# Log-forget running sum placed first in the order, w_in handed out later and shared by two blocks, V's high part on ScalarE

## The chip, the cores and the metric

The kernel runs on one core of a Trainium2 chip. The metric is device time of one execution in microseconds (us); it is the median of several runs. The engines are TensorE (PE, with its weight loads as PEld), VectorE (DVE), ScalarE (ACT), GpSimd (POOL) and SyncE (SP). SP's queue issues nearly all DMAs here. Every engine and every queue works through its own instructions in a fixed order, and an instruction that waits holds all that stand behind it.

## The reference

Attention with a decay, then two feed-forward layers, all in float32 (the weights are kept as float64 pairs and decoded on the chip):

```python
# q, k, v: (4, 8, 576, 64); f: (4, 8, 576)
scores = q @ k.T / sqrt(64)
cum = cumsum(log(clip(f, 1e-4, 1)), -1)
scores = where(causal, -1e9, scores + cum[:, :, :, None] - cum[:, :, None, :])
x = softmax(scores) @ v               # reshaped to 2304 tokens x 512
h = x @ w_in                          # 512 x 2048
y = (h * tanh(softplus(h))) @ w_out   # 2048 x 512
g = maximum(y @ w1, y @ w2, y @ w3)   # 512 x 768 each
out = g @ w_out2                      # 768 x 512
```

## The kernel before, in words

Every large product is done in three matmuls of split values (high x high, high x low, low x high; `mm3`). `split` makes the high part by a rounding copy on a named engine and the low part by a subtraction on another.

**Attention** goes over 16 pairs of heads; each pair has two *units* (`g` = 0 for query rows 0 to 255, `g` = 1 for rows 256 to 575). Here the 32 units are counted 0 to 31, so that pair p has units 2p and 2p+1. `load` issues the DMAs of a pair (q, k, v into `rawq`, `rawk`, `rawv`, one buffer each, and the running sum `cum_d`, spread over partitions, into `cb`). `prep` splits them and turns q and k by PE transposes (`tr`). `scores` makes matmuls into `sc`, then one DVE instruction each (L391) that adds the decay and takes the minimum (`mn`), an exponential on ACT (L397), and a scaling of P on POOL (L404). `av`, which runs one unit later, turns P (`pp`), splits it into TA or TB and multiplies by V; its sums go by way of `xt` (L453) and an SP DMA (L461) to the DRAM tensors `x_d`. A pair's `prep` stands between the two units of the pair before.

**The running sum** is made once: f is loaded into `fl` (L122), clipped (L125), its logarithm taken on ACT (L126), summed along the row on DVE (L128), scaled (L129) and stored as `cum_d` (L130). Every `cb` load reads `cum_d`.

**w_in** is loaded by a generator, `load_w_in`: 16 half column groups, two to a group `fp` of 256 columns. A half group is two DMAs into `wr` (L149), one ACT instruction (L152), four DVE instructions (L155, L158, L161, L165, 64 in all), the high part on ACT (L135) and the low part on POOL (L141). Two staging buffers (`wt`, `wr`) hold them.

**h** = x w_in is done in 72 steps, each one block of 256 tokens (`i`, 9 of them) by one column group (`fp`, 8 of them), 24 matmuls a step. A block can start when its tokens of all heads are stored; blocks 0 and 1 become ready in the course of units 6 to 8, block 6 only near the end of attention.

The order of instructions is set by the tile scheduler. The loop at L535 calls the attention generator once per unit under `tc.high_priority(AHEAD)`, then hands out one half group of w_in, then up to four h steps. What has higher priority is put first where it fits.

When attention is over, its SBUF is given to w_out (`wo`), which is decoded on DVE while the last 24 h steps run; then come y and the second layer.

Of the kernel before, what the change touches and what calls it, by code (L numbers as in the profile page):

```python
# [9 lines left out]
F32 = mybir.dt.float32  # L10
# [3 lines left out]
AF = mybir.ActivationFunctionType  # L14
ALU = mybir.AluOpType
# [16 lines left out]
AHEAD = 3000  # L32
# [35 lines left out]
def tile_decay_attention__mish_ff__max3_ff(  # L68
# [16 lines left out]
    nc = tc.nc  # L85
    B, H, S, D = q.shape
# [3 lines left out]
    NH = B * H  # L90
    KD = DM // 128
    NFP = DFF // 256
    NF2 = DFF2 // 128
    NBLK = NT // BLK
    scale = 1.0 / float(D) ** 0.5
# [8 lines left out]
    cum_d = dram.tile([NH, S], F32, name="cum_d")  # L104
# [7 lines left out]
    with tc.tile_pool(name="setup", bufs=1) as sp:  # L112
        maskf = sp.tile([128, 128], F32, name="maskf")
        nc.gpsimd.memset(maskf, 0.0)
        nc.gpsimd.affine_select(
            out=maskf, in_=maskf, pattern=[[-1, 128]], compare_op=ALU.is_ge,
            fill=-1e30, base=0, channel_multiplier=1,
        )
        for rows, cols in ((slice(0, 64), slice(0, 64)), (slice(64, 128), slice(64, 128))):
            nc.vector.tensor_copy(mask4[rows], maskf[rows, cols])  # L120
        fl = sp.tile([NH, S], F32, name="fl")
        nc.sync.dma_start(fl, f.rearrange("b h s -> (b h) s"))  # L122
        one = sp.tile([NH, S], F32, name="one")
        nc.vector.memset(one, 1.0)
        nc.vector.tensor_scalar(fl, fl, 1e-4, 1.0, op0=ALU.max, op1=ALU.min)  # L125
        nc.scalar.activation(fl, fl, AF.Ln)  # L126
        cum = sp.tile([NH, S], F32, name="cum")
        nc.vector.tensor_tensor_scan(cum, one, fl, 0.0, op0=ALU.mult, op1=ALU.subtract)  # L128
        nc.vector.tensor_scalar(cum, cum, 1.0 / scale, None, op0=ALU.mult)  # L129
        nc.sync.dma_start(cum_d[:], cum)  # L130
        nc.scalar.preload_act_table_set("natural_log_exp_and_others")

    def split(dst_hi, dst_lo, src, eng_hi, eng_lo):
        if eng_hi == "act":
            nc.scalar.activation(dst_hi, src, AF.Copy)  # L135
        elif eng_hi == "pool":
            nc.gpsimd.tensor_scalar(dst_hi, src, 1.0, 1.0, op0=ALU.mult, op1=ALU.mult)
        else:
            nc.vector.tensor_copy(dst_hi, src)
        eng = nc.gpsimd if eng_lo == "pool" else nc.vector  # L140
        eng.tensor_tensor(out=dst_lo, in0=src, in1=dst_hi, op=ALU.subtract)  # L141
# [32 lines left out]
    def mm3(ps, whl, xhl, start, stop):  # L174
        (wh, wl), (xh, xl) = whl, xhl
        nc.tensor.matmul(ps, wh, xh, start=start, stop=False, skip_group_check=True)  # L176
        nc.tensor.matmul(ps, wh, xl, start=False, stop=False, skip_group_check=True)  # L177
        nc.tensor.matmul(ps, wl, xh, start=False, stop=stop, skip_group_check=True)  # L178
# [11 lines left out]
    def load_w_in():  # L190
        for fp in range(NFP):
            fs = slice(fp * 256, fp * 256 + 256)
            for c in range(0, KD, 2):
                blocks = [moe_w_in[d * 128:(d + 1) * 128, fs] for d in (c, c + 1)]
                load_split(
                    wst, wi[fp][:, 0, c:c + 2], wi[fp][:, 1, c:c + 2], blocks, "act", "pool", abs_eng="act"
                )
                yield
            loaded.add(fp)

    def load_x(i):
        xr = xp.tile([128, KD, BLK], F32, name="xr", tag="xr", bufs=1)
        nc.sync.dma_start(xr, x_d[i][:])
        xh = xp.tile([128, KD, BLK], F32R, name="xh")
        xl = xp.tile([128, KD, BLK], F32R, name="xl")
        split(xh, xl, xr, "pool", "pool")
        return xh, xl
# [9 lines left out]
    def att_psum(name):  # L217
        return aps.tile([128, 512], F32, name=name, tag="ps", bufs=4)
# [5 lines left out]
    raw = [ap_.tile([128, 640 if c == "v" else S], F32, name=f"raw{c}") for c in "qkv"]  # L224

    qk = [ap_.tile([128, 9, 3 - i, 64], F32R, name=f"qk{i}") for i in range(2)]
    vs = [aw.tile([128, 10, 2, 64], F32R, name=f"vs{i}") for i in range(2)]
# [33 lines left out]
                src[b, hs, 512:S, :].rearrange("h p d -> p h d"),  # L261
            )

    def split_raw(t, r):

        split(t[:, :, 0], t[:, :, 1], r.rearrange("p (n d) -> p n d", d=64), "dve", "pool")

    def load(b, hp):

# [39 lines left out]
    def prep(J):  # L309

        qh = as_.tile([128, 2, 512], F32R, name="qh", bufs=2)
        ql = as_.tile([128, 2, 512], F32R, name="ql", bufs=2)
        kk = as_.tile([128, 2, S], F32R, name="kT", bufs=2)
        last = q4[count["prep"] % 2]
        count["prep"] += 1

        def turn(dst, c, src):
            nc.tensor.transpose(dst[:, c:c + 128].bitcast(F32R), src, identr)

        rest = att_psum("tr")  # L320

        split_raw(qk[1], raw[1])
        split_raw(qk[0], raw[0])
        nc.gpsimd.tensor_scalar(
            qk[0][:, :, 2], raw[0].rearrange("p (n d) -> p n d", d=64), 1.0, 1.0, op0=ALU.mult, op1=ALU.mult
        )
        for i, part, dst, n in ((1, 0, kk, 0), (0, 0, qh, 1), (0, 1, ql, 2)):
            src = lambda blk: qk[i][:, blk, part:part + 2, :].rearrange("p a d -> p (a d)")
            for h in range(2):
                tr = att_psum("tr")  # L330
                for c in range(4):
                    turn(tr, c * 128, src(4 * h + c))
                nc.scalar.activation(
                    dst[:, h, 0:512].rearrange("p (c t) -> p c t", t=4),
                    tr.rearrange("p (t c) -> p c t", t=4),
                    AF.Copy,
                )
            turn(rest, n * 128, src(8))
        rr = rest[:, 0:384].rearrange("p (i h c) -> p i h c", i=3, h=2)
        nc.scalar.activation(kk[:, :, 512:S], rr[:, 0], AF.Copy)  # L340
        for a in range(2):
            nc.scalar.activation(
                last[:, a].rearrange("p (a c) -> p a c", c=64)[:, 0:4:3, :], rr[:, 1 + a], AF.Copy
            )
        split_raw(J["vs"], raw[2])
        J.update(q=(qh, ql), q4=last, k=kk)

    def score_mm(J, h, qt, dst, c0, w):
# [142 lines left out]
    def ready(i):  # L491
        return BLK * (i + 1) <= done

    def h_steps():


        half = NFP // 2
        order = [(i, fp) for fp in range(half) for i in (0, 1)]
        order += [(i, fp) for i in (0, 1) for fp in range(half, NFP)]
        order += [(i, fp) for i in range(2, NBLK) for fp in range(NFP)]  # L500
        final = {i: n for n, (i, _) in enumerate(order)}
        xs = {}
        asked = 0
        for n, (i, fp) in enumerate(order):
            while not ready(i):
                yield False

            while asked < NBLK and ready(asked) and asked <= i + 1 and (asked < 2 or n > final[asked - 2]):
                xs[asked] = load_x(asked)
                asked += 1  # L510
            while fp not in loaded:
                next(wgen, None)
            xh, xl = xs[i]
            h = hps.tile([128, 2, BLK], F32, name="h")
            for a in range(2):
                fs = slice(a * 128, (a + 1) * 128)
                for c in range(KD):
                    mm3(
                        h[:, a, :], (wi[fp][:, 0, c, fs], wi[fp][:, 1, c, fs]),
                        (xh[:, c, :], xl[:, c, :]), a == 0 and c == 0, c == KD - 1,  # L520
                    )
            he = hst.tile([128, 2, BLK], F32, name="he")
            if n % 2 and done < NT:
                nc.vector.tensor_copy(he, h)
            else:
                nc.scalar.activation(he, h, AF.Copy)  # L526
            ib, off = divmod(i * BLK, BLK2)
            nc.sync.dma_start(h_d[ib][fp][:, :, off:off + BLK], he)
            yield True

    wgen = load_w_in()
    attn = attention()
    steps = h_steps()
    credit = 0.0
    while True:  # L535

        with tc.high_priority(AHEAD):
            done = next(attn, None)
        if done is None:
            break  # L540
        next(wgen, None)
        credit += RATE
        while credit >= 1.0:
            credit -= 1.0
            if not next(steps, False):
                credit = 0.0
# [69 lines left out]
    for step, (ib, fp, a) in enumerate(todo):  # L616
        n = blocks1[ib][1]
# [103 lines left out]
```

## Time and profile before

| | us |
|---|---|
| median of 3 runs | 1052.75 (1051.04 to 1054.09) |
| profiled execution | 1048.8 |
| its span | 1047.0 |
| PE busy in the span | 958.4 |
| DVE busy | 524.3 |
| ACT busy | 415.4 |
| POOL busy | 381.0 |

The profiled execution is a little faster than the three timed ones. Its time is 1.8 us longer than its span. A busy time is a sum over stages that have different limits, so the stages have to be looked at one by one.

### The profile page before, as it was taken

The numbers are of one execution on the slowest core, as the hardware profiler recorded it, in microseconds if no ns is written. First come the engines' busy times: TensorE is split into PE (matmuls) and PEld (weight loads), VectorE is DVE, ScalarE is ACT, GpSimd is POOL, SyncE is SP. The second block draws the span as 40 slices with busy tenths as digits, with TensorE's granted clock in tenths as the row PEclk, the third lists the DMA queues.
The fourth block names the chain that finished last, engine by engine and source line by source line (L and its number), as shares of the span: only waits on it lengthen the run. The fifth ranks groups of instructions, "written<-read, shape, count | busy, mean of one in ns | idle before, by whom it ended". The sixth has DMA issues, their size and how long they took to land.

```text
span 1047.0 us, 15897 instructions
## 1 busy us (share of the span) xinstructions
PE 958.4 (92%) x5756; PEld 848.4 (81%) x5756; DVE 524.3 (50%) x1119; ACT 415.4 (40%) x920; POOL 381.0 (36%) x437
## 2 busy tenths in 40 slices
PE   2666779999998999999699989998999999999998
PEld 2555669999998999899688778777988888888886
DVE  5898854565556555578865775653211111112110
ACT  2667655655655655542124344433221211211111
POOL 5766665445644652255433333330111001011010
PEclk9887789999999899989999999998999999999999
DMA  5654443445443431285644665543300100200101
GB/s 150 200 157 137 132 132 103 129 118 161 136 127 123 121 117 63 78 301 183 191 136 161 208 194 172 191 147 111 105 22 0 61 21 1 71 11 1 41 0 41
DMA packets 106446, 119.16 MB, mean 114 GB/s; under 512 B 33984, under 2 KB 79552, under 8 KB 106368
## 3 DMA queue, kind: packets, MB, share of 16 engines
q1 hardware_dynamic: 106368, 118.15, 36.2%
q8 instruction: 45, 0.74, 0.3%
q14 instruction: 33, 0.27, 0.1%
HBM read 85.01 MB, written 33.10 MB: 113 GB/s over the span
## 4 chain that ended last, share of the span: by engine, by line
PE 56%; DMA 17%; DVE 16%; POOL 4%; issue 3%; SPq 2%; ACT 2%; POOLq 0%; DVEq 0%; ACTq 0%
PE g L178 7%; PE g L177 7%; PE g L176 7%; DMA wr<-in_moe_w_dram 5%; DMA wr<-in_moe_w_out_dram 4%; PE av L436 4%; PE h L176 4%; PE h L177 4%; DMA cb<-cum_d 4%; PE pp L423 4%; PE h L178 4%; PE sc L356 3%; DVE wt L161 3%; PE o L176 2%; PE o L178 2%
## 5 line engine op out<-in xcount | busy, mean ns | idle before, releaser
L176 PE MATMUL h<-xh,wi 128*128 128x256 f32 x576 | 167.5, 292 | 9.9 <-ACT he L526 8.5
L177 PE MATMUL h<-xl,wi 128*128 128x256 f32 x576 | 167.8, 291 | 1.9 <-POOL xl L141 1.9
L178 PE MATMUL h<-xh,wi 128*128 128x256 f32 x576 | 167.0, 290 | 0.0
L141 POOL TENSOR_TENSOR hl<-mx,hh 128x512 fp32r<-128x512 f32 x27 | 36.4, 1349 | 278.7 <-ACT hh L135 278.7
L177 PE MATMUL g<-yl,wm 128*128 128x512 f32 (+1 forms) x360 | 134.8, 374 | 0.0
L176 PE MATMUL g<-yh,wm 128*128 128x512 f32 (+1 forms) x360 | 134.7, 374 | 0.0
L178 PE MATMUL g<-yh,wm 128*128 128x512 f32 (+1 forms) x360 | 134.6, 374 | 0.0
L176 PE MATMUL y<-gh,wo 128*128 128x512 f32 (+1 forms) x320 | 118.2, 373 | 5.8 <-ACT gh L135 4.6
L177 PE MATMUL y<-gl,wo 128*128 128x512 f32 (+1 forms) x320 | 119.3, 374 | 3.3 <-DVE gl L141 3.1
L176 PEld LDWEIGHTS h<-xh,wi 128*128 128x128 f32 x576 | 111.3, 194 | 11.2 <-ACT he L526 8.7
L178 PE MATMUL y<-gh,wo 128*128 128x512 f32 (+1 forms) x320 | 118.1, 371 | 0.0
L177 PEld LDWEIGHTS h<-xl,wi 128*128 128x128 f32 x576 | 111.9, 194 | 3.1 <-POOL xl L141 2.1
L178 PEld LDWEIGHTS h<-xh,wi 128*128 128x128 f32 x576 | 111.8, 194 | 0.7
L607 ACT ACTIVATE g<-g 128x512 f32<-128x512 f32 (+1 forms) x80 | 46.8, 588 | 128.9 <-DMA g<-h_d 110.7
L677 DVE TENSOR_TENSOR mx<-g,mx 128x512 f32<-128x512 f32 x27 | 18.7, 693 | 156.2 <-PE g L178 156.2
L423 PE MATMUL pp<-ident,P 128*128 128x128 f32 x320 | 71.9, 321 | 23.0 <-POOL P L404 21.8
L397 ACT ACTIVATE P<-P,mn 128x128 f32<-128x128 f32 (+3 forms) x128 | 71.3, 558 | 48.7 <-DVE mn L391 48.0
L177 PEld LDWEIGHTS g<-yl,wm 128*128 128x128 f32 x360 | 68.2, 190 | 13.2
L178 PEld LDWEIGHTS g<-yh,wm 128*128 128x128 f32 x360 | 68.2, 189 | 13.1
L176 PEld LDWEIGHTS g<-yh,wm 128*128 128x128 f32 x360 | 68.2, 189 | 13.0
L404 POOL TENSOR_SCALAR P<-P,rr 128x256 f32<-128x256 f32 (+3 forms) x128 | 69.2, 559 | 23.9 <-ACT vlo L444 11.0
L141 DVE TENSOR_TENSOR gl<-g,gh 128x512 fp32r<-128x512 f32 (+1 forms) x80 | 60.9, 766 | 33.0 <-ACT gh L135 32.5
(101 smaller groups left out, 1995.9 us busy)
## 6 DMA issues: line engine op xcount, KB each, us to landing
h_d<-he SPq DMA_DIRECT2D x72, 256.0 KB, 3.3
g<-h_d SPq DMA_DIRECT2D x64, 256.0 KB, 3.2
wr<-in_moe_w_out_dram SPq DMA_DIRECT2D x22, 512.0 KB, 4.1
wr<-in_moe_w_dram SPq DMA_DIRECT2D x24, 384.0 KB, 3.2
wr<-in_moe_w_in_dram SPq DMA_DIRECT2D x32, 256.0 KB, 3.1
cb<-cum_d SPq DMA_DIRECT2D x64, 128.0 KB, 3.3
cb<-cum_d SPq DMA_DIRECT2D x32, 144.0 KB, 3.7
xr<-x_d SPq DMA_DIRECT2D x9, 512.0 KB, 3.7
```

Of the source, the lines that this page charges most:

```text
L141: eng.tensor_tensor(out=dst_lo, in0=src, in1=dst_hi, op=ALU.subtract)
L161: nc.vector.scalar_tensor_tensor(out=ti, in0=hi, scalar=-0x40000000, in1=ti, op0=ALU.bitwise_and, op1=ALU.bitwise_or,)
L176: nc.tensor.matmul(ps, wh, xh, start=start, stop=False, skip_group_check=True)
L177: nc.tensor.matmul(ps, wh, xl, start=False, stop=False, skip_group_check=True)
L178: nc.tensor.matmul(ps, wl, xh, start=False, stop=stop, skip_group_check=True)
L356: nc.tensor.matmul(o, lhs, rhs, start=n == 0, stop=n == len(mms) - 1, skip_group_check=True)
L397: nc.scalar.activation(Pt, Pt, AF.Exp, scale=-1.0, bias=mn[:, cl:cl + 1], accum_out=sm[:, ci:ci + 1],)
L404: nc.gpsimd.tensor_scalar(Pt, Pt, rr[:, ci:ci + 1], 1.0, op0=ALU.mult, op1=ALU.mult)
L423: nc.tensor.transpose(pp[:, n * 128:n * 128 + 128], Pt[:, k0:k0 + 128], ident)
L436: nc.tensor.matmul(avp[h][:, off:off + w], vl, T[:, i, c:c + w], start=kt == 0 and i == 0 and not (g == 0 and h == 1), stop=last and i == ...
L607: nc.scalar.activation(g, g, AF.Mish)
L677: nc.vector.tensor_tensor(out=mx, in0=g[1], in1=mx, op=ALU.max)
```

## The change

Four edits. The running sum's instructions get the highest priority of all. w_in is handed out two half groups at a time in calls 7 to 14 of the loop (call n+2 carries unit n) in place of one in every call from the first; h steps may still ask for a group earlier. The first six column groups of blocks 0 and 1, in place of the first four, alternate between the two blocks. V's high part is made by ACT in place of DVE.

```diff
-        fl = sp.tile([NH, S], F32, name="fl")
-        nc.sync.dma_start(fl, f.rearrange("b h s -> (b h) s"))
...
-        nc.sync.dma_start(cum_d[:], cum)
+        with tc.high_priority(2 * AHEAD):
+            fl = sp.tile([NH, S], F32, name="fl")
+            nc.sync.dma_start(fl, f.rearrange("b h s -> (b h) s"))
+            one = sp.tile([NH, S], F32, name="one")
+            nc.vector.memset(one, 1.0)
+            nc.vector.tensor_scalar(fl, fl, 1e-4, 1.0, op0=ALU.max, op1=ALU.min)
+            nc.scalar.activation(fl, fl, AF.Ln)
+            cum = sp.tile([NH, S], F32, name="cum")
+            nc.vector.tensor_tensor_scan(cum, one, fl, 0.0, op0=ALU.mult, op1=ALU.subtract)
+            nc.vector.tensor_scalar(cum, cum, 1.0 / scale, None, op0=ALU.mult)
+            nc.sync.dma_start(cum_d[:], cum)
...
-    def split_raw(t, r):
+    def split_raw(t, r, eng="dve"):
 
-        split(t[:, :, 0], t[:, :, 1], r.rearrange("p (n d) -> p n d", d=64), "dve", "pool")
+        split(t[:, :, 0], t[:, :, 1], r.rearrange("p (n d) -> p n d", d=64), eng, "pool")
...
-        split_raw(J["vs"], raw[2])
+        split_raw(J["vs"], raw[2], "act")
...
-        half = NFP // 2
+        half = NFP - 2
...
-    credit = 0.0
+    credit, na = 0.0, 0
     while True:
...
-        next(wgen, None)
+
+        na += 1
+        for _ in range(2 if 7 <= na <= 14 else 0):
+            next(wgen, None)
```

In the changed program the lines behind L121 have a number higher by one (by four behind the loop).

**SP's queue at the start.** Before, the load of f and the store of the sum stand behind the loads of two pairs and of part of a third (`raw*` are q, k and v, `wr` is w_in):

```order
L122 DMA fl<-in_f_dram 32x576
L149 DMA wr<-in_moe_w_in_dram 128x512 x2
L247 DMA rawq<-in_q_dram 128x2x256
...
L247 DMA rawq<-in_q_dram 128x2x256
L252 DMA rawq<-in_q_dram 64x64 x2
L255 DMA rawv<-in_v_dram 128x4x64 x2
L259 DMA rawv<-in_v_dram 64x2x64
L130 DMA cum_d<-cum 32x576
L149 DMA wr<-in_moe_w_in_dram 128x512 x2
L281 DMA cb<-cum_d 128x256
```

Now the queue begins like this:

```order
L123 DMA fl<-in_f_dram 32x576
L248 DMA rawk<-in_k_dram 128x2x256
L253 DMA rawk<-in_k_dram 64x64 x2
L248 DMA rawq<-in_q_dram 128x2x256
L253 DMA rawq<-in_q_dram 64x64 x2
L256 DMA rawv<-in_v_dram 128x4x64
L131 DMA cum_d<-cum 32x576
L256 DMA rawv<-in_v_dram 128x4x64
L260 DMA rawv<-in_v_dram 64x2x64
L282 DMA cb<-cum_d 128x256
```

The sum and the `cb` loads of the first pair have moved ahead of the loads of the second pair, which now come behind them; the first w_in load stands behind the `x_d` store of unit 0.

**DVE at the start and in unit 1.** Before, the start of DVE's program reads (`qk_188` and `qk_187` are split k and q, `vs` split V, `identr` what the transposes need, `mask` a causal mask):

```order
L139 CAST qk_188<-rawk 128x9x64
L139 CAST qk_187<-rawq 128x9x64
L109 CAST identr<-ident 128x128
L120 CAST mask_122<-maskf 64x64 x2
L139 CAST vs_189<-rawv 128x10x64
L139 CAST qk_188<-rawk 128x9x64
L125 TENSOR_SCALAR fl<-fl 32x576
L128 SCALAR_TENSOR_TENSOR cum<-one,fl 32x576
L129 TENSOR_SCALAR cum<-cum 32x576
```

and now:

```order
L126 TENSOR_SCALAR fl<-fl 32x576
L129 SCALAR_TENSOR_TENSOR cum<-one,fl 32x576
L140 CAST qk_188<-rawk 128x9x64
L130 TENSOR_SCALAR cum<-cum 32x576
L109 CAST identr<-ident 128x128
L120 CAST mask_122<-maskf 64x64 x2
L140 CAST qk_187<-rawq 128x9x64
L392 ISA P_0_311,mn<-sc,cb 128x128
```

q's cast now stands behind the sum and behind the two mask casts. Further down, in the scores of unit 1, before (`wt` is w_in):

```order
L391 ISA P_0_418,mn<-sc,cb 128x384
L391 ISA mn 128x1
L391 ISA P_0_424,mn<-sc,cb 128x512
L391 ISA mn 128x1
L155 TENSOR_SCALAR wt<-wt 128x512
L391 ISA P_1_430,mn<-sc,cb 128x384
L391 ISA mn 128x1
L158 TENSOR_SCALAR wt<-wt 128x512
L391 ISA P_1_436,mn<-sc,cb 128x512
L391 ISA mn 128x1
L161 SCALAR_TENSOR_TENSOR wt<-wr,wt 128x512
L155 TENSOR_SCALAR wt<-wt 128x512
```

and now:

```order
L140 CAST qk_188<-rawk 128x9x64
L392 ISA P_0_396,mn<-sc,cb 128x384
L392 ISA mn 128x1
L140 CAST qk_187<-rawq 128x9x64
L392 ISA P_0_402,mn<-sc,cb 128x512
L392 ISA mn 128x1
L392 ISA P_1_408,mn<-sc,cb 128x384
L392 ISA mn 128x1
L392 ISA P_1_414,mn<-sc,cb 128x512
L392 ISA mn 128x1
L392 ISA P_None,mn<-sc,cb_225 128x288
L392 ISA mn 128x1
```

The w_in instructions have gone from these scores, and the casts of the pair after next (pair 2) stand there.

**SP's queue at the end of attention.** Before (`x_d_68` is the last store of attention, `xr` the load of a block of x for h):

```order
L461 DMA x_d_67<-xt_5869 128x64
L461 DMA x_d_68<-xt_5869 128x256
L203 DMA xr<-x_d_67 128x1024
L149 DMA wr<-in_moe_w_out_dram 128x1024
L149 DMA wr<-in_moe_w_out_dram 128x1024
```

and now:

```order
L462 DMA x_d_67<-xt_5845 128x64
L462 DMA x_d_68<-xt_5845 128x256
L150 DMA wr<-in_moe_w_out_dram 128x1024
L204 DMA xr<-x_d_67 128x1024
L150 DMA wr<-in_moe_w_out_dram 128x1024
```

The first load of w_out has moved ahead of the load of block 7. Over the whole program, counted in the order of each engine:

| ahead of the end of unit | 1 | 3 | 5 | 7 | 9 | 10 |
|---|---|---|---|---|---|---|
| w_in instructions on DVE (of 64), before | 26 | 44 | 59 | 64 | 64 | 64 |
| now | 6 | 20 | 33 | 44 | 59 | 64 |

| h steps on PE ahead of the end of unit | 9 | 14 | 15 | 21 | 22 | 29 | 31 |
|---|---|---|---|---|---|---|---|
| before | 1.5 | 14.0 | 16.0 | 30.4 | 32.0 | 46.2 | 48.0 |
| now | 1.3 | 15.0 | 16.1 | 31.0 | 32.0 | 47.0 | 48.0 |

From the end of unit 31 on, PE's program is the same in both.

## Rows read from the trace of the kernel before

**Rows 1.** Page, part 1: busy time, share of the span, instructions.

```profile
PE 958.4 (92%) x5756; PEld 848.4 (81%) x5756; DVE 524.3 (50%) x1119; ACT 415.4 (40%) x920; POOL 381.0 (36%) x437
```

**Rows 2.** Windows of 25 us: busy us and instructions by engine, granted clock, DMA.

```profile
50.00:75.00 25.00, 18.28 (x102) 14.73 (x100) 24.38 (x55) 17.20 (x44) 16.13 (x16) 0.84 0.48 137
...
125.00:150.00 25.00, 21.91 (x139) 19.63 (x137) 16.40 (x48) 16.32 (x44) 16.66 (x20) 0.80 0.38 113
...
275.00:300.00 25.00, 25.00 (x213) 24.82 (x212) 13.80 (x41) 14.93 (x39) 10.82 (x18) 1.00 0.41 126
```

**Rows 3.** Timeline, first 30 us: start, duration (us), engine, instruction, idle before.

```profile
0.73 0.44 SPq L247 DMA_DIRECT2D rawk<-in_k_dram  x1
...
5.89 0.75 DVE L139 CAST qk<-rawq 128x576 fp32r<-128x576 f32 x1 [1.17 <-DMA rawq<-in_q_dram]
...
6.97 2.62 DVE L120 CAST mask<-maskf 64x64 bf16<-64x64 f32 x2 [0.19 <-POOL maskf L115]
...
9.62 0.50 DVE L139 CAST vs<-rawv 128x640 fp32r<-128x640 f32 x1
...
10.70 1.38 DVE L125 TENSOR_SCALAR fl<-fl 32x576 f32<-32x576 f32 x1
...
13.32 0.58 PE L356 MATMUL sc<-kT,qh 128*128 128x256 f32 x1 [1.40 <-ACT qh L333]
...
14.58 0.74 DVE L129 TENSOR_SCALAR cum<-cum 32x576 f32<-32x576 f32 x1
...
29.25 0.29 DVE L391 CUSTOM_DVE_ANT_0 P<-sc,cb 128x128 f32<-128x128 f32 x1 [0.90 <-POOL cb L284]
```

**Rows 4.** The chain of waits, 0 to 66 us: start, us, what held the chain.

```profile
21.91 2.06 DMA cum_d<-cum
...
24.04 0.33 SPq L281
...
33.97 1.73 PE sc L356 x4
```

**Rows 5.** Timeline, ends of units 1, 3, 5, 7 (SP's stores) and 9 (DVE).

```profile
63.59 0.81 SPq L461 DMA_DIRECT2D x_d<-xt  x2
...
94.51 0.81 SPq L461 DMA_DIRECT2D x_d<-xt  x2
...
120.28 0.89 SPq L461 DMA_DIRECT2D x_d<-xt  x2
...
143.86 0.80 SPq L461 DMA_DIRECT2D x_d<-xt  x2
...
167.66 0.61 DVE L453 TENSOR_TENSOR xt<-av,vlo 64x64 f32<-64x64 f32 x3
```

**Rows 6.** Groups of instructions on DVE, 8 to 130 us: busy us, mean ns.

```profile
L165 DVE SCALAR_TENSOR_TENSOR wt<-wr,wt 128x512 int32<-128x512 int32 x16 | 14.3, 893 | 0.1
L161 DVE SCALAR_TENSOR_TENSOR wt<-wr,wt 128x512 int32<-128x512 int32 x16 | 13.8, 863 | 0.1
L158 DVE TENSOR_SCALAR wt<-wt 128x512 int32<-128x512 int32 x16 | 12.5, 781 | 0.2
...
L155 DVE TENSOR_SCALAR wt<-wt 128x512 f32<-128x512 f32 x16 | 8.6, 536 | 9.0 <-ACT wt L152 9.0
...
L139 DVE CAST vs<-rawv 128x640 fp32r<-128x640 f32 x5 | 5.2, 1044 | 0.1
```

**Rows 7.** Groups of instructions on ACT, 8 to 130 us.

```profile
L135 ACT ACTIVATE wi<-wt 128x512 fp32r<-128x512 f32 x16 | 10.1, 629 | 17.0 <-DMA cum_d<-cum 8.8 <-DVE wt L165 8.1
```

**Rows 8.** Who waited for whom, PE, 140 us to the end: us, times, longest.

```profile
PE pp L423 <- POOL P L404: 9.4, 7, 4.0
PE h L176 <- ACT he L526: 8.5, 1, 8.5
```

**Rows 9.** The chain of waits, 436 to 450 us.

```profile
444.03 2.35 POOL xl L141
...
446.81 4.56 DMA wr<-in_moe_w_out_dram
```

More of the change, by code (lines that the diff above doesn't have):

```diff
@@ L120, in tile_decay_attention__mish_ff__max3_ff @@
             nc.vector.tensor_copy(mask4[rows], maskf[rows, cols])
-        fl = sp.tile([NH, S], F32, name="fl")
-        nc.sync.dma_start(fl, f.rearrange("b h s -> (b h) s"))
[L123 to L129, printed above, removed]
-        nc.sync.dma_start(cum_d[:], cum)
+        with tc.high_priority(2 * AHEAD):
[9 more added lines that the diff above has]
+            nc.sync.dma_start(cum_d[:], cum)
         nc.scalar.preload_act_table_set("natural_log_exp_and_others")
```

## The prediction

> **What bounds the kernel now.** I read the page's busy times first, then windows of 25 us, then the chain of waits, then the timelines of the first 170 us. PE is busy for 958.4 of 1047.0 us [rows 1], so the profile's page alone says that PE is the bound and that a change to loads and casts is worth little. The windows say otherwise for the beginning: from 50 to 75 us PE is busy for 18.28 of 25 us at a granted clock of 0.84, while DVE is busy for 24.38; from 275 to 300 us PE is busy throughout at 1.00 and DVE for only 13.80 [rows 2]. So the first 170 us, eight to ten units of attention with no h step to fill PE, are paced by other engines, and behind them PE is nearly full: from 140 us on it waits only for some 9.4 us on P and once for 8.5 us [rows 8]. What a change takes from the first 170 us is therefore kept, unless it is given back in one of these later waits.
>
> In the first 170 us the reader is to see two things. The first score reaches DVE at 29.25 us, though the first score matmul starts at 13.32 [rows 3]: between them the chain goes through the store of `cum_d`, issued at 21.91, and the `cb` loads from 24.04 [rows 4]. DVE had the sum ready at 15.32 (14.58 + 0.74); the store waited 6.6 us in SP's queue behind loads of later pairs. Second, the ends of units 1, 3, 5, 7 and 9 lie at 63.6, 94.5, 120.3, 143.9 and 168.3 us [rows 5]: a pair takes 30.9, 25.8, 23.6 and 24.4 us, and in these four stretches DVE has 18, 15, 5 and 0 instructions of w_in.
>
> **The change part by part.**
>
> *A, the sum first.* Two things must now be ready for the first score. One is `cb`. f is issued in the place of the first load, 0.73 us; with the 2.06 us of the store of `cum_d` as its landing [rows 3, 4] it is there at about 2.8. From the clip to the end of the scale it took 4.6 us (10.70 to 15.32), and the cast of k (0.75) now stands in between: 8.2. The store lands 2.1 later, and from the first `cb` load to the first score on DVE it took 5.2 us (24.04 to 29.25) [rows 3, 4]: 15.5. The other is q. Its cast now stands behind the scale and the two mask casts (2.62 us [rows 3]): it starts at about 10.9. From q's cast to the first score matmul it took 7.4 us (5.89 to 13.32), and two matmuls of 0.58 more to the first score's end: 19.4. But in these 7.4 us ACT held q's copies behind the logarithm, which now comes long before; the idle time ahead of the matmul, 1.40 us [rows 3], shows at least that much, and on an otherwise empty DVE the clip and the masks should be shorter. I take 16.9, between the two and nearer to the first. Gain 12.4 us, bounds 9.9 and 13.8.
>
> *B, units 0 and 1 without w_in.* By the order 26 w_in instructions stood ahead of the end of unit 1, and now 6. One costs DVE 0.77 us ((14.3 + 13.8 + 12.5 + 8.6) / 64 [rows 6]). What of that lies on the path I read from the pairs: 18 against 5 instructions is 30.9 against 23.6 us, 0.56 us each; 15 against 5 is 0.22 each [rows 5]. So 20 fewer are worth 11.2 us (4.4 to 15.4). Against it stand two new waits. The loads of pair 1's k and q now come behind `cb`: twelve issues at some 0.45 us [rows 3] from 10.4 on, q's last is issued at about 16, lands at 18, and its preparation (7.4 us as above) ends at 25.4; PE has unit 1's scores queued behind those transposes. That is 8.5 us behind the first score, where it was 4.7 (29.25 to 33.97 [rows 3, 4]): 3.8 lost. And DVE now has pair 2's casts among unit 1's scores; the one of q waits for a load that can only be issued when pair 1's q has been split: one landing, 2.1. Sum of B: 11.2 - 5.9 = 5.3 us gained, bounds 1.5 lost and 9.5 gained.
>
> *C, units 2 to 9.* Now 14, 13, 11 and 15 w_in instructions stand in the four pairs. Pairs with 15 took 25.8 us, with 5, 23.6 [rows 5]; so I give them 25.6, 25.3, 24.9 and 25.9, together 101.7 against 104.7 before. Gain 3 us. If each of the 15 instructions more (53 against 38) costs 0.56, it is a loss of 8; the bound on the other side is 6 gained. The cast of V is in it: it leaves DVE and costs ACT about 0.63 us (0.629 for 512 columns [rows 7]), which is hidden, since ACT is busy for only 17.20 of 25 us [rows 2].
>
> V's cast took 0.50 us at 9.62, where POOL stood idle, and 1.044 in the mean of five [rows 3, 6]; the five cost 2.5 us of DVE by the short duration and 5.2 by the mean. The Trainium skill, "SBUF — State Buffer", section "Who interferes with whom", says that VectorE in certain modes and GpSimd take one pair of SBUF ports in turn, each for a whole instruction, and that ScalarE has ports of its own. By that rule the long casts were waits that ScalarE will not have, C would be 2.7 us better and the time 1032; by the short row alone it stays at 1034.
>
> *D, h steps that run ahead.* In the order h is 1.0 step ahead at unit 14, 0.6 at unit 21, and 0.8 at unit 29, and then must wait for the same blocks. A step is 24 matmuls; PE does 213 in 25 us where it is full [rows 2], so 2.8 us. At units 22 and 23 and at units 30 and 31 PE then has 0.6 and 0.8 steps less to fill with, where it already waits for P [rows 8]: 3.9 us lost, at the least none. The sharing itself removes and adds no instruction. w_in is not late for h: 59 of 64 instructions stand ahead of unit 9's end, and the steps done by then use group 0 alone.
>
> *E, w_out's first load.* It was issued at 446.81 behind a load of x that waited for POOL's 2.35 us [rows 9]; it now stands ahead of that load. From there to the end of h the w_out load is what the h stores queue behind. Gain 2 us, at the least none.
>
> Sum: 12.4 + 5.3 + 3.0 - 3.9 + 2.0 = 18.8 us. The profiled execution took 1048.8 us, so it would be 1030.0. The median of the runs is 3.95 above the profiled one; the forecast for the median is 1052.75 - 18.8 = 1034.0.
>
> **The rivals.**
>
> *w_in was on the path in full.* Each of its 20 instructions in units 0 and 1 is worth 0.77 us, V's five casts are worth their mean (2.7 more in C), and h running ahead costs half: 12.4 + 15.4 - 5.9 + 5.7 - 2 + 2 = 27.6 us, 1025. For it: DVE at 24.38 of 25 [rows 2]. Against it: the pair with 5 instructions took only 2.2 us less than the one with 15.
>
> *Only the sum counts.* Units are held by `cb`, SP's queue and POOL's order, not by DVE: B is its lower bound, 1.5 lost, C nothing, D as above, E nothing: 12.4 - 1.5 - 3.9 = 7.0 us, 1046. For it: the same 2.2 us, and POOL at 16 to 17 us in both early windows [rows 2].
>
> *The load returns as h starts (slower).* In units 6 to 10 31 w_in instructions now stand where 5 stood, and DVE holds P, x and the first h copies behind them. 26 more, each at a price on the path, stand against 12.4 + 5.3 + about 4 of units 2 to 5, less the 3.9 of D: 17.8 us. It turns at 0.68 us each; at 0.77 it is 2.2 us slower, at the longest of the means, 0.89 [rows 6], 5.4 us: 1058. Against it: DVE is busy for only 16.40 of 25 us from 125 to 150 us [rows 2].
>
> *The change does nothing.* The first score is held by q until close to 29 us and B fails: within 3 us of before. Nothing in the rows speaks for it; q's path would have to be 10 us longer.
>
> **How the numbers follow.** Forecast 60 in 100, w_in in full 16, only the sum 16, slower 5, nothing 3. The first three are faster by more than 0.3% (3.2 us), about what a measurement can tell from no change: 0.92 faster, 0.03 same, 0.05 slower. The range takes in the first two rivals: 1023 to 1046.
>
> **What would show it.** A: the first L392 on DVE at about 17 us. B: unit 1's `x_d` store at about 46 us, pair 1's transposes at 20 to 25. C: unit 9's end at about 148 us, pairs of 25 to 26 us. D: the waits of PE for P longer by 2 us at units 22 and 23, and again before the end of attention. E: the first w_out load right behind the last `x_d` store, some 19 us earlier than 446.8. It would be wrong if P or `xt` waits in units 6 to 9 for w_in on DVE, or if the second and third pair's loads hold units 1 to 3 by more than 6 us.

## The result

| | before | after |
|---|---|---|
| median of the runs made together | 1053.42 (1051.04 to 1055.08) | 1038.31 (1036.30 to 1042.16) |
| profiled execution | 1048.8 | 1036.78 |
| its span | 1047.0 | 1034.9 |

The ratio is 0.9879, 95% interval 0.985 to 0.9907: faster by a little over 1%, some 15 us between the medians, 12.1 us between the two spans of the profiled executions, which all stages below are read from. The forecast was 1034.0 in 1023 to 1046, with 18.8 us between the profiled executions. The direction and the range hold; between the profiled executions 6.7 us of the sum are missing.

### The profile after

The page's busy times answer to [rows 1]; they say as little as before:

```profile
PE 957.5 (93%) x5756; PEld 844.8 (82%) x5756; DVE 509.5 (49%) x1103; ACT 425.6 (41%) x936; POOL 379.9 (37%) x437
```

The timeline of the first 15 us, to be read against [rows 3] (start, duration, engine, instruction, idle time before and what ended it):

```profile
2.60 0.45 DVE L126 TENSOR_SCALAR fl<-fl 32x576 f32<-32x576 f32 x1 [1.10 <-DMA fl<-in_f_dram]
...
6.17 0.34 SPq L131 DMA_DIRECT2D cum_d<-cum  x1
...
7.41 0.89 DVE L120 CAST mask<-maskf 64x64 bf16<-64x64 f32 x2
7.92 0.40 SPq L282 DMA_DIRECT2D cb<-cum_d  x1
8.33 0.75 DVE L140 CAST qk<-rawq 128x576 fp32r<-128x576 f32 x1
...
12.95 0.76 PE L357 MATMUL sc<-kT,qh 128*128 128x256 f32 x2
...
14.30 0.29 DVE L392 CUSTOM_DVE_ANT_0 P<-sc,cb 128x128 f32<-128x128 f32 x1 [5.22 <-PE sc L357]
```

The first score is on DVE at 14.30 where it was at 29.25, and it now waits for PE's scores, no longer for `cb`. The ends of units 1, 3, 5 and 7 (SP's stores), of unit 9 (DVE) and of unit 10 (SP), and the last store of attention with the first w_out load behind it, from the timeline, against [rows 5, 9]:

```profile
46.47 0.47 SPq L462 DMA_DIRECT2D x_d<-xt  x1
...
70.51 0.81 SPq L462 DMA_DIRECT2D x_d<-xt  x2
...
96.98 0.81 SPq L462 DMA_DIRECT2D x_d<-xt  x2
...
121.48 0.80 SPq L462 DMA_DIRECT2D x_d<-xt  x2
...
149.88 1.10 DVE L454 TENSOR_TENSOR xt<-av,vlo 64x320 f32<-64x320 f32 x4
...
163.47 0.80 SPq L462 DMA_DIRECT2D x_d<-xt  x2
...
430.40 0.80 SPq L462 DMA_DIRECT2D x_d<-xt  x2
431.30 0.37 SPq L150 DMA_DIRECT2D wr<-in_moe_w_out_dram  x1
```

In the kernel before, the end of unit 10 and the last store of attention read

```profile
184.11 0.80 SPq L461 DMA_DIRECT2D x_d<-xt  x2
...
444.05 0.80 SPq L461 DMA_DIRECT2D x_d<-xt  x2
```

The lead over before is 15.0 us at the first score, 17.1 at unit 1, 24.0 at unit 3, 23.3 at unit 5, 22.4 at unit 7, then only 17.3 at unit 9, but 20.6 again at unit 10. At the end of attention it is 13.7, at the end of h (534.8 before, 521.8 after) 13.0, at the end of the span 12.1. So more was gained early than forecast, and it was given back at two places. One is units 8 and 9, which take 29.5 us (121.48 to 150.98) where they took 24.4; two thirds of this is made good by the end of unit 10. The other, and the larger one, is behind unit 10: 6.9 us. Windows of 25 us (busy time of PE, PEld, DVE, ACT, POOL, then granted clock and DMA), against [rows 2]:

```profile
50.00:75.00 25.00, 18.95 (x108) 15.46 (x107) 22.01 (x56) 18.95 (x48) 19.42 (x22) 0.84 0.52 148
...
125.00:150.00 25.00, 19.90 (x129) 18.13 (x130) 21.85 (x45) 16.95 (x42) 19.33 (x22) 0.80 0.47 145
...
225.00:250.00 25.00, 22.38 (x163) 22.07 (x163) 10.02 (x35) 12.68 (x34) 13.14 (x15) 0.86 0.50 150
250.00:275.00 25.00, 25.00 (x212) 24.82 (x211) 13.89 (x38) 15.30 (x38) 13.98 (x18) 1.00 0.44 132
```

From 125 to 150 us DVE has 21.85 us of work where it had 16.40: w_in's decoding now lies there. From 225 to 250 us PE does 163 matmuls where a full window has 212. The chain of waits there (start, us, what held the chain):

```profile
219.14 4.07 DMA x_d<-xt
223.27 3.96 DMA xr<-x_d
227.27 0.11 issue
227.38 1.06 POOL xh L138
228.44 0.04 issue
228.48 0.50 PE h L177 x2
...
235.65 0.21 PE h L179
235.87 0.19 PE h L177
236.06 0.12 PE h L178
```

The first h step of block 2 stands ahead of attention's matmuls on PE, and PE waits 2.62 us for its x, which has just gone out to DRAM and come back. Behind the wait an h matmul takes 0.21 us until 235.9 and 0.12 us from then on; the granted clock of the window is 0.86. By an estimate from these rows the 2.6 us wait cost some 6 us (49 matmuls of 0.12 us fewer than in a full window): to the wait come some 7 us, 229 to 236 us, at a granted clock of 0.50 to 0.54, the lower of the two levels.

### The profile page after: what moved, and what is told of

Same layout as the page of the kernel before. It is cut to its first block, busy times and chain, and to the rows that moved or that the text cites. A ratio compares the mean times of both kernels' runs of the same rounds, so it can differ in the third digit from the quotient of the medians.

```text
span 1034.9 us, 15873 instructions
## 1 busy us (share of the span) xinstructions
PE 957.5 (93%) x5756; PEld 844.8 (82%) x5756; DVE 509.5 (49%) x1103; ACT 425.6 (41%) x936; POOL 379.9 (37%) x437
## 4 chain that ended last, share of the span: by engine, by line
PE 54%; DMA 18%; DVE 17%; issue 4%; ACT 3%; POOL 3%; SPq 2%; DVEq 0%; POOLq 0%; ACTq 0%
PE g L179 7%; PE g L178 7%; PE g L177 7%; DMA wr<-in_moe_w_dram 5%; PE h L177 4%; PE h L178 4%; PE h L179 4%; DMA wr<-in_moe_w_out_dram 4%; DVE wt L162 3%; PE av L437 3%; PE pp L424 3%; PE sc L357 3%; DMA cb<-cum_d 3%; PE o L177 2%; PE o L179 2%
## 5 line engine op out<-in xcount | busy, mean ns | idle before, releaser
L405 POOL TENSOR_SCALAR P<-P,rr 128x128 f32<-128x128 f32 (+3 forms) x128 | 68.0, 550 | 25.7 <-DVE rr L403 12.5
L177 PEld LDWEIGHTS y<-gh,wo 128*128 128x128 f32 x320 | 61.3, 192 | 18.4 <-ACT gh L136 6.4
```

Source lines behind the costliest of these rows:

```text
L405: nc.gpsimd.tensor_scalar(Pt, Pt, rr[:, ci:ci + 1], 1.0, op0=ALU.mult, op1=ALU.mult)
```

## The experiments

The place to read a kernel by turned out to be the end of attention. "Behind" is the span less that time; all columns but the first two are of the profiled execution. Each ratio is to the kernel before, run together with it (its median was 1051.2 to 1052.3 us beside e1 to e12).

| kernel | median, us | ratio, 95% | end of attention | end of h | span | behind |
|---|---|---|---|---|---|---|
| before | 1053.42 | | 444.05 | 534.8 | 1047.0 | 603.0 |
| after | 1038.31 | 0.9879 (0.985 to 0.9907) | 430.40 | 521.8 | 1034.9 | 604.5 |
| e1 sum alone | 1051.35 | 0.9995 (0.9975 to 1.0014) | 437.96 | 523.4 | 1050.2 | 612.2 |
| e2 all but the sum | 1053.33 | 1.0017 (0.9996 to 1.0037) | 439.40 | 525.9 | 1052.7 | 613.3 |
| e3 all but the hand-out | 1040.85 | 0.9903 (0.9877 to 0.9929) | 427.45 | 513.5 | 1040.4 | 613.0 |
| e4 all but V | 1047.71 | 0.9963 (0.9944 to 0.9981) | 435.92 | 520.1 | 1048.3 | 612.4 |
| e5 before, w_in not decoded | 1033.45 | 0.9827 (0.9804 to 0.9849) | 428.53 | 520.3 | 1033.2 | 604.7 |
| e6 sum alone, w_in not decoded | 1023.83 | 0.973 (0.9707 to 0.9754) | 410.56 | 495.9 | 1023.0 | 612.4 |
| e7 V alone | 1057.81 | 1.006 (1.0038 to 1.0082) | 443.35 | 528.0 | 1054.1 | 610.8 |
| e8 x in two parts | 1038.42 | 0.9876 (0.9853 to 0.9899) | 432.14 | 506.9 | 1034.9 | 602.8 |
| e9 hand-out at calls 2 to 9 | 1035.77 | 0.9841 (0.9821 to 0.986) | 428.25 | 518.6 | 1034.5 | 606.3 |
| e10 hand-out at calls 3 to 10 | 1046.76 | 0.9945 (0.9924 to 0.9965) | 431.16 | 515.6 | 1040.8 | 609.6 |
| e11 no sum, calls 3 to 10 | 1048.89 | 0.9981 (0.9963 to 0.9999) | 445.78 | 535.8 | 1048.6 | 602.8 |
| e12 e9 with q's cast on ScalarE | 1045.62 | 0.9945 (0.9923 to 0.9967) | 431.19 | 528.2 | 1043.0 | 611.8 |

### One edit at a time (e1 to e4)

Theory 1 was the prediction's: the early sum carries nearly all of it. e1 has the sum's block of the diff and nothing else. e2 has the other three edits. e3 and e4 undo one edit of the changed kernel each:

```diff
# e3: one half group in every call, as before
-        for _ in range(2 if 7 <= na <= 14 else 0):
-            next(wgen, None)
+        next(wgen, None)
# e4: V's high part on VectorE, as before
-        split_raw(J["vs"], raw[2], "act")
+        split_raw(J["vs"], raw[2])
```

e1: 

> The kernel before with the sum's high priority alone; w_in's hand-out, the column groups and V's cast as before. By the order w_in is out of units 0 and 1 here too (6 DVE instructions ahead of the end of unit 1, as with all four edits, against 26), because DVE no longer has idle time there for lower priority to fill. Theory 1, the sum carries everything: 1038 us, +-3, first score at about 14.3 us, unit 7 ending within 2 us of 122. Rival, the later hand-out carries the w_in part: 1044 us or more, 3 to 5 us behind the kernel with all four edits. h is 14.2 steps on at unit 14, not 15.0; if running ahead costs what the trace of the changed kernel suggests (6 us at block 2), this kernel is the faster one by up to 6.

e2: 

> The changed kernel without the sum's high priority; the other three edits stay. By the order w_in stands in units 0 and 1 as before (16 and 26 instructions). Theory 1: 1053 us, +-3, first score near 29 us. Rival, the other edits carry a part of their own: 1047 us or less.

e3: 

> The changed kernel with w_in handed out as before; sum, groups and V as changed. Counts of w_in are nearly those of the changed kernel (6, 18, 31, 43, 60 at units 1, 3, 5, 7, 9), but h is further ahead (4.7 steps at unit 9, 16.0 at unit 14). Theory 1: within 3 us of 1038; with h a step further ahead at block 2 rather 1 to 3 us slower than faster. Rival, the later hand-out is worth 4 us or more by itself: 1042 us or more.

e4: 

> The changed kernel with V's high part back on DVE. Theory 1, worth nothing that can be seen: 1038 us, +-2. Rival, V's casts were on the path of DVE with their mean of about a microsecond in ten units: 1041 to 1043.

Theory 1 fell: e2 and e3 came as it says (1053.33 and 1040.85), but e1 is 13 us above its forecast, its unit 7 ends at 134.4 us and not near 122, and e4 is above both of its own. The sum alone makes no difference to the time that can be measured, although its unit 0 ends 15.7 us earlier (32.1 us on DVE for 47.8), as in the changed kernel. By unit 9 (165.1 us on DVE) 3.2 us of that are left, where the changed kernel has 17.3. The three other edits without the sum are worth nothing in the time either. Without V's edit the gain is 4 us, without the hand-out it is 10 to 12 (of 13 to 15; by ratio and by medians). So most of the gain is there only with the sum and V's cast in one kernel. The edit of the column groups has no run of its own; with the sum, it and the hand-out together are worth 2.0 us by the end of attention (e1 against e4). V's casts of the first seven pairs, by tile (ns shortest/median/longest, first and last start), in e4:

```profile
L140 DVE CAST vs<-rawv x7: 1454/1706/1725, 9.5 to 157.6; 128x640 fp32r<-128x640 f32 x7
```

and in the changed kernel:

```profile
L136 ACT ACTIVATE vs<-rawv x7: 719/730/740, 9.5 to 145.6; 128x640 fp32r<-128x640 f32 x7
```

On VectorE the same cast takes 0.50 us where POOL stands idle [rows 3] and up to 1.73; on ScalarE all seven are within 0.02 us of each other.

### Where the sum's gain goes (e5, e6) and V alone (e7)

Theory 2: in units 1 to 9 VectorE's work is the bound. Before, part of w_in's decoding filled its idle time ahead of the first score; the early sum takes that time away, and the decoding comes back in units 2 to 9. To test it, e5 and e6 leave out three of the four VectorE instructions that decode a piece of w_in, in the kernel before and in e1:

```diff
         nc.vector.tensor_scalar(
             t, t, F32_MIN_AS_HIGH_HALF, F32_MAX_AS_HIGH_HALF, op0=ALU.max, op1=ALU.min
         )
+        if abs_eng == "act":
+            return t
```

e5: 

> The kernel before with three of the four VectorE instructions that decode each piece of w_in left out (so w_in is not decoded here, and h is computed from other numbers); it is the partner of the next run. Theory 2 (VectorE's time is the bound up to unit 9, and the decoding fills its idle time ahead of the first score): with the sum late, 26 of 64 decoding instructions lay in units 0 and 1, so leaving 48 out frees at most some 14 us of units 0 and 1 (20 instructions of about 0.8 us) but the wait for the sum to 29.25 us stays; 1040 us, 1035 to 1047. Rival (order and queues, not VectorE's time): 1049 to 1053.

e6: 

> The sum moved, and nothing else, with the same three of four decoding instructions left out (w_in is not decoded here). Theory 2: with the decoding gone there is nothing that the early sum pushes into units 2 to 9, so its 15 us show: 10 to 15 us below the run before it in this call, with unit 9's end at least 10 us earlier than there, where with the decoding in place the sum alone was worth 1 us and unit 9 ended 3 us earlier. Rival (the order of the queues eats the gain): no more than 4 us below.

e7 is the kernel before with V's edit alone: 

> The kernel before with nothing changed but V's high part on ScalarE. Theory 2: V's casts of pairs 1 to 5 leave VectorE (5 of 1.2 us in its trace between 30 and 175 us), which is bound there also in the kernel before: 1046 us, 1043 to 1050, about 6 us faster, so that sum (1) and V (6) together give less than both in one kernel (12). If the sum and V simply add (no interaction), V alone must give 11 us: 1041. Rival (V's cast matters only for the order of the queues once the sum is early): 1050 to 1053.

The last store of attention in the timeline of e5:

```profile
428.53 0.80 SPq L463 DMA_DIRECT2D x_d<-xt  x2
```

and of e6:

```profile
410.56 0.80 SPq L464 DMA_DIRECT2D x_d<-xt  x2
```

Without the decoding the early sum is worth 18.0 us at the end of attention, with it 6.1 (444.05 to 437.96). Unit 9 ends at 151.6 us in e5 and at 134.9 in e6, on DVE. What eats most of the sum's gain is thus w_in's decoding: by the end of attention leaving out three quarters of it saves 15.5 us with the late sum (444.05 to 428.53) and 27.4 with the early one (437.96 to 410.56). From 100 to 125 us, by windows, e1 has

```profile
100.00:125.00 25.00, 17.09 (x76) 12.90 (x76) 22.29 (x53) 15.95 (x39) 18.89 (x23) 0.73 0.64 186
```

and e6

```profile
100.00:125.00 25.00, 21.65 (x147) 18.57 (x147) 19.52 (x55) 20.28 (x53) 21.19 (x26) 0.93 0.55 160
```

The total showed only 9.6 of these 18.0 us (1033.45 to 1023.83), just less than the 10 to 15 expected, and e5 itself came out 1.5 us below its range. e7 missed all three of its expectations: 5.5 us slower, although attention ends 0.7 us earlier. The column "behind" holds the rest: some 603 to 605 us in the kernels before and after and in e5, but 611 to 613 in all the others up to here. That is Theory 4.

### Two lengths behind attention (e9 to e11)

How the rows behind attention stand is set by the scheduler over the whole program. In the traces PE's last 2,958 matmuls stand in the same order in the kernels before and after and in e5, e9 and e11; e1 to e4, e6, e7 and e10 share another order there, from the last h steps on. An edit at unit 1 can so change the order at 500 us. The two lengths go with the two orders in every trace: in the first, h ends 90.0 to 91.9 us behind attention and y takes 207 to 211 us from there; in the second, 84.2 to 86.5 and 220 to 223. From the end of y on, all take 305 us. e9 and e10 differ from the changed kernel, and from each other, in one number:

```diff
# e9 (e10: 3 and 10; e11: as e10, with the sum where it was before)
-        for _ in range(2 if 7 <= na <= 14 else 0):
+        for _ in range(2 if 2 <= na <= 9 else 0):
```

e9: 

> The changed kernel with w_in handed out at calls 2 to 9 in place of 7 to 14. Theory 4 (the time is that of attention's end plus a tail, and the tail has two lengths by the order in which the rows behind attention stand: 603 to 605 us in the kernels before and after, 611 to 613 us in the five that had parts of the change alone, where the second product waits 8 to 11 us for VectorE's gl): here the rows behind attention stand as in the changed kernel and those of units 0 to 9 nearly as in the kernel without the late hand-out, so attention ends at 427 to 431 us, the tail is 603 to 605 us, and the time is 1035 us, 1032 to 1038. Rival (the hand-out itself saves the 2.5 us that leaving it out cost): 1039 to 1042.

e10: 

> The same with calls 3 to 10, one call later. The rows of units 0 to 9 differ little from those of the run before it, but behind attention they stand as in the kernels with parts of the change alone. Theory 4: attention ends at 427 to 431 us, the tail is 611 to 613 us, PE waits 8 us or more for gl behind 440 us, and the time is 1042 us, 1040 to 1045, some 8 us above the run before it. Rival (one call of hand-out cannot matter, the tails differ by what attention leaves to do): within 3 us of the run before it.

e11: 

> The kernel with V's cast on ScalarE, the groups and the hand-out at calls 3 to 10, but the sum where it was before; behind attention its rows stand as in the kernels before and after. Theory 4 with Theory 2: V's cast without the sum is worth 1 to 5 us at attention's end (439 to 443 us), the tail is 603 to 605 us, so 1048 us, 1046 to 1051: V alone did not lose 5 us by itself, its tail did. Rival (ScalarE's casts cost time of their own when the sum is late): attention's end at 444 us or later, 1053 or more.

e9 came as expected, with 606.3 us behind attention for 603 to 605. e9 is 1035.77 us, e10 1046.76, above its range: 11 us apart. The two profiled executions are only 6.3 us apart, 2.9 of it by the end of attention and 3.3 behind it (609.6 us, a little below what was expected); e10's (1042.6 us) is at the low end of its runs, 1042.0 to 1049.4, and no trace shows where its longer runs lose the rest. PE's waits from 440 to 760 us (total, times, longest) in e9:

```profile
PE h L177 <- ACT he L527: 7.2, 1, 7.2
PE y L177 <- ACT gh L136: 5.1, 4, 2.0
PE y L178 <- DVE gl L142: 4.6, 4, 1.4
```

and in e10:

```profile
PE y L178 <- DVE gl L142: 9.4, 9, 2.3
PE y L177 <- ACT gh L136: 6.0, 6, 2.0
PE h L177 <- ACT he L527: 2.9, 4, 1.2
```

In the one order PE waits once for 7 us in the last h steps, for `he` that stands on ACT behind a `g` that has not landed. In the other it does not, and its h ends 84.4 us behind attention rather than 90.4; but then y waits nine times for `gl`, which stands on DVE between the decoding of the next weights, and takes 220.1 us from the end of h to its own end where e9 takes 210.8. Since e9 and e10 have the same instructions, the order is the cause of these 3.3 us.

e11 shows that e7's loss lay there too: 1048.89, and 602.8 us behind attention, as expected. Its attention ended at 445.78, not at 439 to 443: without the sum, V's cast (with this hand-out) brings nothing. e2 differs from e11 in nothing but the calls (7 to 14) and ended attention at 439.40, 6.4 us earlier; why the calls make so much there is open.

### Two tries that gained nothing (e8, e12)

e8 loads and splits the x of a block in two parts, so that h of block 2 needs the last pair's chunk last. It aims at the wait at 228 us, then called Theory 3:

```diff
-        nc.sync.dma_start(xr, x_d[i][:])
+        nc.sync.dma_start(xr[:, 0:3], x_d[i][:, 0:3])
+        nc.sync.dma_start(xr[:, 3:4], x_d[i][:, 3:4])
...
-            for a in range(2):
-                fs = slice(a * 128, (a + 1) * 128)
-                for c in range(KD):
+            for c in range(KD):
+                for a in range(2):
+                    fs = slice(a * 128, (a + 1) * 128)
```

> The changed kernel, with x of each block of h loaded and split in two parts (three of its four chunks first, the last behind it), and the loop over chunks outside that over halves of h, so that the last pair's chunk is used last. Theory 3 (of the 20 us that the changed kernel is ahead at unit 10, 6 are given back at 225 to 236 us, by the 2.62 us wait for block 2's x and the half clock behind it): no wait for xh over 1 us near 228 us, a granted clock of 0.95 or more there, and 1033 us, 1030 to 1036. Rival (the lead is lost to something else there, the wait only sits on top of it): 1037 to 1040, with another wait at the same place.

Two windows of e8:

```profile
100.00:125.00 25.00, 17.62 (x78) 13.97 (x78) 19.46 (x51) 15.69 (x38) 16.91 (x21) 0.69 0.62 179
225.00:250.00 25.00, 25.00 (x212) 24.80 (x212) 13.90 (x41) 15.86 (x39) 13.52 (x18) 1.00 0.44 131
```

The wait is gone and the clock is at 1.00, but the time (1038.42) is that of the rival, and as much was lost ahead of the wait: the first h steps now stand at units 7 to 9, and PE did 78 matmuls from 100 to 125 us where it did 126 in the changed kernel. The run does not show what the wait cost. e9 does so better: there h is 0.8 steps less ahead at unit 14, the wait is gone as well (its window from 225 to 250 us has PE at 25.00 and the clock at 1.00), and attention ends 2.15 us earlier, though unit 10 ended 3.1 us later (166.5 for 163.4 on DVE).

e12 is e9 with q's high part on ScalarE too (`split_raw(qk[0], raw[0], "act")`): 

> The kernel with the hand-out at calls 2 to 9, and q's high part on ScalarE as well. Theory 2 (in units 1 to 9 VectorE's time is the bound, so what leaves it is gained): five casts of 0.74 us leave VectorE between 30 and 155 us, so unit 9 ends 2 to 4 us earlier than without it (149 us where it was 152.7) and attention at 424 to 427 us where it was 428.3. Rival (q's cast, unlike V's, stands ahead of the transposes of its pair, and ScalarE gets to it behind its own work): unit 9 at 152 us or later. The rows behind attention stand in a third order, whose tail is not known; by Theory 4 it is 603 to 613 us, so 1029 to 1042 us in all.

The rival was right: unit 9 ends later (157.2 us on DVE for 152.6), attention 2.9 us later, and the time is 1045.62, above its range. PE's waits from 175 to 440 us for P, in e12:

```profile
PE pp L424 <- POOL P L405: 7.7, 6, 4.8
```

where e9 has 4.3 us in four waits. On PE 5.3 h steps stand ahead of unit 9's end there, for 1.0 in e9. So "what leaves VectorE is gained" is too simple, and Theory 2 holds for w_in's decoding, not for every cast.

## Why the prediction was right, and where its sum was not

**A, the sum first: right, too small.** Forecast 12.4 us, first score at 16.9; measured 15.0, at 14.30. `cb` came sooner than forecast: f landed by 2.60 (2.8 forecast), but the sum was ready at 6.15 (8.2), and the first `cb` load went out at 7.92 (10.3). q's path held the first score, as forecast, and there the term was mis-sized. The two mask casts took 0.89 us, not the 2.62 of [rows 3], and from q's cast to the first score matmul it took 4.6 us (8.33 to 12.95), not 7.4. The cast of `identr`, which also stands ahead of q's, is not in the forecast; it took 1.41 us.

**B, units 0 and 1 without w_in: right in kind, too large.** Forecast 5.3, measured 2.2 (17.1 less 15.0). It is no edit of its own: in e1's trace, too, 0 and 6 w_in instructions stand ahead of the ends of units 0 and 1. The early sum moves them by itself (unit 1 ends at 50.9 us there, on DVE, for 46.4).

**C, units 2 to 9: wrong at unit 9, right at unit 10.** Forecast 3.0, measured 0.2 by unit 9 (17.3 less 17.1) and 3.5 by unit 10 (20.6 less 17.1). The first three pairs took 24.0, 26.5 and 24.5 us, 75.0 together for 75.8 forecast. Units 8 and 9 took 29.5 for 25.9, in the stretch that holds 15 w_in instructions where none stood; the price on the path was read from pairs 1 to 3 and was too low there. One of the forecast's signs of being wrong did show: the chain of waits to unit 9's end goes through w_in on DVE (L162, 1.15 us at 148.14, ahead of the last `xt`). That is the mechanism of the rival "the load returns as h starts", with 3.6 us where that rival needs more than 17.8.

In C stood the rule on V's casts (the Trainium skill, "SBUF — State Buffer", section "Who interferes with whom"). The trace agrees with it: 0.72 to 0.74 us on ScalarE whatever POOL does, and on VectorE (before, e1, e4, e5 and e6, 80 casts) 0.48 to 0.50 us in all 11 that began with POOL idle, while all 62 that began with more than 0.16 us of a POOL instruction to go ended 0.34 to 0.36 us behind that instruction (seven had less to go). One of them, in e4:

```profile
127.32 1.81 POOL L142 TENSOR_TENSOR qk<-rawk,qk 128x576 fp32r<-128x576 f32 x1 [2.56 <-DVE qk L140]
127.76 1.73 DVE L140 CAST vs<-rawv 128x640 fp32r<-128x640 f32 x1
```

The 2.7 us that the forecast set on this make its time 1031, not the 1032 that it gives. Without V's edit attention ends 5.5 us later (e4).

**D, h steps that run ahead: the loss is there, its place and form wrong.** Forecast 3.9, measured 3.6 from unit 9 (17.3 less 13.7), but 6.9 from unit 10 (20.6 less 13.7), where PE has done about 5 steps in both kernels; that 3.6 is so close to 3.9 is luck. It was to show as longer waits for P at units 22 and 23; the longest there is 3.64 us where it was 3.54. It came at block 2, as the wait for x and the half clock behind it, and e9, with h 0.8 steps less ahead there, does not have it. In the form that was forecast it shows in e3: with all 16 steps of blocks 0 and 1 done by unit 14, PE waits 3.38 us for P at 221.5.

**E, w_out's first load: the load right, the gain wrong.** Forecast 2.0; the load is 15.5 us earlier where attention ends 13.7 earlier, so 1.9. But the end of h is only 13.0 earlier and the span 12.1, so behind attention 1.6 are lost: the last h steps wait for `he` behind `g`, 7.7 us in one wait (8.5 before [rows 8]), not for w_out. This is the sentence that failed: the w_out load is not what the end of h waits for.

The sum, by unit 9: 18.8 + 2.6 (A) - 3.1 (B) - 2.8 (C) + 0.3 (D) - 3.6 (E) = 12.2, against 12.1 measured. By unit 10, C is + 0.5 and D - 3.0.

What the prediction did not see at all is that its terms do not add. It says that what is taken from the first 170 us is kept unless it is given back in a later wait. By the end of attention the sum alone keeps 6.1 us, V alone 0.7, sum and V (with the groups) 16.6. That V's casts, up to 1.7 us each on VectorE, are part of this is argued; e12 shows that moving a cast is no gain by itself, and which of V's time, V's place in the order and the column groups makes the 10 us is open. Nor did it see that the late hand-out, at the end of attention, costs 3.0 us (427.45 in e3, 430.40 after), and that the whole kernel is no slower with it (0.9879 for 0.9903, and the intervals overlap) only because the order behind attention stayed that of before: 604.5 us there, 613.0 in e3. That was luck, and no part of the forecast.

The fastest kernel is e9: 0.9841 of before, sure; its lead over the changed kernel is 2.5 us between the medians and 4 by the ratios, but the two intervals overlap, so that it is not shown.

## What to carry to other kernels

A gain at the start of a kernel whose second engine is nearly full can be only lent, as here: look for the work that used to fill the wait, since it has to be done somewhere. Where a scheduler sets the order, read each variant at a milestone that its edit can reach, and the rest by itself; here an edit at the start changed the time behind attention by 9 us (603.0 before, 612.2 in e1). And run edits in pairs as well as alone: two that kept 6.1 and 0.7 us by the end of attention kept 16.6 together (with the column groups).

## What the runs showed of the hardware

A 2.62 us wait of PE cost more than twice its length, by the estimate above. Behind it the granted clock was 0.50 to 0.54 from 229 to 236 us, the lower of its two levels, with h matmuls 0.21 us apart, and then 1.00, with 0.12 us:

```profile
232.00:236.00 4.00, 4.00 (x20) 4.00 (x20) 0.89 (x4) 1.36 (x4) 3.81 (x4) 0.51 0.39 115
...
240.00:244.00 4.00, 4.00 (x36) 4.00 (x35) 2.04 (x8) 2.54 (x8) 0.00 (x0) 1.00 0.64 158
```

And one VectorE cast of 128 x 640 took between 0.48 and 1.73 us in these kernels, by what was left of the POOL instruction beside it (0.34 to 0.36 us more than that, in 62 of 62 casts), while the same cast on ScalarE took between 0.72 and 0.74.
